# A long convolution with gated projections on one core: a hand-written order replaced by a list scheduler, with the head's products taken from PSUM, six first-stage groups set aside and late gating of four chunks

## The chip, the core and the metric

The kernel runs on one core of a Trainium2 chip. TensorE (PE) multiplies, with its weight loads shown as a row of their own (PEld); VectorE (DVE), ScalarE (ACT) and GpSimd (POOL) work on elements; SyncE (SP) issues the transfers, which 16 DMA engines carry out. Matmul results land in PSUM, eight banks of 128 x 512 numbers; everything else lies in SBUF. Each engine takes its own instructions in program order. The metric is device time in microseconds (us) of one execution. All data is 32-bit float.

## The reference

For 8 batches of 6400 steps and 128 channels: a causal convolution of each channel with a filter as long as the sequence (by FFT in the reference), a five-tap causal convolution of the result whose sigmoid is a gate, a projection, the gating, and a second projection.

```python
L = 2 * S
Xf = np.fft.rfft(x, n=L, axis=1)
Hf = np.fft.rfft(h, n=L, axis=0)
y = np.fft.irfft(Xf * Hf[None, :, :], n=L, axis=1)[:, :S, :]
...
for k in range(K):
    gate_pre += conv_w[k][None, None, :] * xp[:, k:k + S, :]
gate = 1.0 / (1.0 + np.exp(-gate_pre))
val = x @ w_val
return (gate * val @ w_out).astype(np.float32)
```

In the last lines `x` is the convolution's `y`, and `xp` is it with four zero steps in front. The transfer of a batch in and out is 3.3 MB each way.

## The kernel before

The 6400 steps are laid out as 100 x 64, and the Fourier transform is done as four stages of matmuls.

- **First stage** (`Forward.group`, 16 groups of 8 channels a batch): four matmuls of 128x200 against `r1_sb`, from an input tile `x`. Four copies of 64x400 bring the result from PSUM to `gy` (for the filter `h` to `gh`, which lies in `dt`).
- **Second stage** (`s2_mm`, 13 blocks `kb` of 8 frequencies, the last of 4): a matmul of 128x128 per frequency against the loaded `m2`. `Product` multiplies by the filter's spectrum: `swap` brings the swapped parts to `w` (two ACT instructions, one with the sign), `mul_u` and `mul_t` (DVE) multiply by the two spectrum tiles `h`, and `add` sums into `gy` (POOL; the last block on DVE).
- **Third stage** (`s3_quad`, 32 quads of 4 channels): four matmuls of 128 columns from `gy` against `r3_sb`, and one copy of 100x512 to `dt`, on ACT and DVE in turn.
- **Fourth stage** (`Chunk`, 13 chunks: the head chunk of 4 columns, and 12 of 5): two matmuls of 100 columns per column from `dt` against `m4_sb`, into one bank. From that bank `copies` (ACT) takes the result `y`, the first tap into the gate's cells (in `dt` or `gl`) and a scaled copy `p`; `taps` adds three taps on DVE and one on POOL. Then `project` (one matmul of up to 500 columns from `y`), `sigm` (ACT), `gate` (DVE), `output` (a second matmul, from the gated cells) and `store`: a copy to `y` and a transfer out.

The **head** of the program does the first stage for `h` and for batch 0, and then their second stages in turn. There `Spectrum` copies each block of the filter's spectrum twice (ACT the real part, DVE the imaginary part) to tiles of 128 partitions, which the product uses and which are stored to HBM (`hd`); for blocks from `LATER` = 7 on only half is stored, and `h_double` copies it to the other half later.

Then each batch `b` runs its third stage, with the first stage of batch `b + 1` beside it (two quads, then a group), and its fourth stage, with the second stage of batch `b + 1` beside it: in step `s` of the loop at L551 chunk `s` and block `s + 1`. A chunk is projected two steps after it is made; what is left of a batch at the end (`trail`, L583) is done in the first rounds of the next third stage. The order on each engine is the order of the calls, which `_InOrder` keeps. PSUM is two pairs of banks and four single banks (before the first batch: four pairs). All transfers are issued by SP, in the order of the calls.

Of the kernel before, what the change touches and what calls it, by code (L numbers as in the profile page):

```python
# [15 lines left out]
C = 128  # L16
# [17 lines left out]
LATER = 7  # L34
# [3 lines left out]
XB = 4  # L38

# [60 lines left out]

@with_exitstack
def longconv_moe(ctx: ExitStack, tc: tile.TileContext, x, h, r1, m2, r3, m4, w64, out):
# [6 lines left out]
    ps2 = ctx.enter_context(tc.tile_pool(name="ps2", bufs=2, space=bass.MemoryType.PSUM))  # L109
    psp = tc.tile_pool(name="psp", bufs=2, space=bass.MemoryType.PSUM)  # L110
    pairs = [ps2, psp.__enter__()]
# [5 lines left out]
    m4_sb = cp.tile([PX, N2 + 1, N1], F32, name="m4_sb")  # L117
# [5 lines left out]
    yl = {a: cp.tile([128, n, N1], F32, name=f"yl_{a}") for a, n in CHUNKS if a >= LATE}  # L123
# [4 lines left out]
    p_t = [cp.tile([128, CH, N1], F32, name=f"p_{i}") for i in range(2)]  # L128
    hd = dp.tile([NKB, 2, 2 * N2, KB * C], F32, name="hd")

    def weights():
        ti = gl.rearrange("p n t -> p (n t)")[:, : 3 * NW].bitcast(I32)
        tf = gl.rearrange("p n t -> p (n t)")[:, 3 * NW : 6 * NW]
        nc.sync.dma_start(ti[:, : 2 * NW], w64.bitcast(I32))
        w = ti[:, : 2 * NW].rearrange("p (n two) -> p two n", two=2)
        lo, hi = w[:, 0], w[:, 1]
        a = ti[:, 2 * NW :]
        f, g = tf[:, :NW], tf[:, NW : 2 * NW]
        b = tf[:, 2 * NW :].bitcast(I32)
        v = nc.vector  # L140

        def bits(o, i, s, p):
            v.tensor_scalar(out=o, in0=i, scalar1=s, scalar2=None, op0=p)

        yield
        bits(a, lo, 28, ALU.logical_shift_right)
        yield
        bits(a, a, 15, ALU.bitwise_and)
        yield
        bits(b, hi, (1 << 20) - 1, ALU.bitwise_and)  # L150
        yield
        v.tensor_copy(g, b)
        yield
        bits(b, a, 1, ALU.logical_shift_right)
        yield
        bits(a, a, 1, ALU.bitwise_and)
        yield
        v.tensor_copy(f, a)
        yield
        v.scalar_tensor_tensor(out=g, in0=g, scalar=8.0, in1=f, op0=MUL, op1=ALU.add)  # L160
        yield
        v.tensor_copy(f, b)
        yield
        v.tensor_tensor(out=g, in0=g, in1=f, op=ALU.add)
        yield
        v.tensor_scalar(out=g, in0=g, scalar1=2.0**-23, scalar2=1.0, op0=MUL, op1=ALU.add)
        yield
        bits(a, hi, 20, ALU.logical_shift_right)
        yield
        bits(a, a, 2047, ALU.bitwise_and)  # L170
        yield
        v.tensor_copy(f, a)
        yield
        v.tensor_scalar(out=f, in0=f, scalar1=-896.0, scalar2=0.0, op0=ALU.add, op1=ALU.max)
        yield
        v.tensor_scalar(out=f, in0=f, scalar1=255.0, scalar2=None, op0=ALU.min)
        yield
        v.tensor_copy(a, f)
        yield
        bits(a, a, 23, ALU.logical_shift_left)  # L180
        yield
        bits(b, hi, 31, ALU.logical_shift_right)
        yield
        bits(b, b, 31, ALU.logical_shift_left)
        yield
        v.tensor_tensor(out=a, in0=a, in1=b, op=ALU.bitwise_or)
        yield
        v.tensor_tensor(out=w_sb, in0=g, in1=a.bitcast(F32), op=MUL)
        yield

    act = nc.scalar.copy
    dve = nc.vector.tensor_copy

    def pair():
        pairs.append(pairs.pop(0))
        return pairs[-1].tile([128, 2, 512], F32, name="pt2", tag="pt2")

    def single():
        return ps1.tile([128, 512], F32, name="pt1", tag="pt1")

    class Forward:


        def __init__(self, src, dst):
            self.src, self.dst, self.n, self.i = src, dst, 0, 0

        def load(self, n=1):
            for _ in range(n):
                if self.n < NG:
                    nc.sync.dma_start(x_sb[self.n % XB], self.src[self.n])  # L210
                    self.n += 1

        def group(self):
            g = self.i
            self.i += 1
            t = x_sb[g % XB]
            pt = pair()
            for m in range(4):
                nc.tensor.matmul(
                    pt[:, m // 2, (m % 2) * SW : (m % 2) * SW + 2 * N1],  # L220
                    lhsT=t[:N1, 2 * m : 2 * m + 2, :].rearrange("p j n -> p (j n)"),
                    rhs=r1_sb,
                    start=True,
                    stop=True,
                )
            self.load()
            v = pt.rearrange("p b (m x) -> p b x m", x=SW)
            return [
                lambda e, j=j, c=c: e(
                    self.dst[c * N2 : (c + 1) * N2, 4 * g + 2 * j : 4 * g + 2 * j + 2],  # L230
                    v[j * N2 : (j + 1) * N2, :, c * N1 : (c + 1) * N1],
                )
                for j in range(2)
                for c in range(2)
            ]

    def count(kb):
        return min(KB, N1 - kb * KB)

    def m2_load(kb):  # L240
        if kb < NKB:
            n = count(kb)
            nc.sync.dma_start(m2_sb[kb % M2B][:, :n], m2[:, kb * KB : kb * KB + n])

    def h_load(kb):
        if kb < NKB:
            n = count(kb) * C
            for r in range(2):
                nc.sync.dma_start(h_sb[(2 * kb + r) % HB][:, :n], hd[kb, r, :, :n])

    def h_double(kb):
        n = count(kb) * C
        for r in range(2):
            nc.sync.dma_start(hd[kb, r, N2:, :n], hd[kb, r, :N2, :n])

    def kdt(t, kb):
        n = count(kb)
        return t[:, : n * C].rearrange("p (d k t) -> p d k t", k=n, t=2)

    def s2_mm(src, kb):  # L260
        pt = pair()
        n = count(kb)
        for k in range(n):
            nc.tensor.matmul(
                pt[:, k // 4, (k % 4) * C : (k % 4 + 1) * C],
                lhsT=m2_sb[kb % M2B][:, k, :],
                rhs=src[:, :, kb * KB + k],
                start=True,
                stop=True,
            )  # L270
        if n <= 4:
            return pt[:, 0, : n * C].rearrange("p (k d t) -> p d k t", t=2, d=C // 2)
        return pt.rearrange("p b (k d t) -> p d (b k) t", t=2, d=C // 2)

    hx = h_sb + [dt[:, N1 * C + i * KB * C : N1 * C + (i + 1) * KB * C] for i in range(2)]

    class Spectrum:
        def __init__(self, kb):
            self.kb, self.v = kb, s2_mm(gh, kb)
            self.h = [hx[(2 * kb + r) % len(hx)] for r in range(2)]  # L280

        def real(self):
            t = kdt(self.h[0], self.kb)
# [346 lines left out]
```

## Time and profile before

| | us |
|---|---|
| median of three runs (1117.69 to 1118.20) | 1117.95 |
| span of the profiled execution | 1115.5 |
| busy: PE, DVE, ACT, POOL | 1053.5, 831.8, 729.7, 410.7 |

The profiled execution's own time is its span and 2.4 us around it, if it ran at the median. The profile gives idle time of an engine with the instruction that released it ("releaser"), groups of instructions by operation and tile (buffer numbers left out, so `pt` is any PSUM tile and `h` any of the spectrum tiles; `m2_sb`, `m4_sb` and `r3_sb` are shown as `m`, `m_sb` and `r_sb`), a timeline in which equal instructions that follow each other are merged ("x16"), and windows: stretches of the span with the busy time of each engine. A matmul of 32-bit floats shows as two records, so that 8 matmuls are x16. All matmul instructions have one line, that of the wrapper at L89, and are told apart by their tiles.

### The profile page before, as it was taken

To read this page: it belongs to the slowest core of one execution; us is meant where nothing else is said; L and a number is where in the kernel's file an instruction comes from. 1 tells how busy PE (TensorE), PEld (TensorE's weight loads), DVE (VectorE), ACT (ScalarE), POOL (GpSimd) and SP (SyncE) were. 2 spreads that over 40 slices of the span, in tenths; PEclk is the share of its full clock that TensorE was granted. 3 is DMA by queue.
4 is the path that set the end of the run, shared out by engine and by line. 5 is a ranking of instruction groups with operands and counts; after the bars stand their busy time and mean duration, and the time that the engine had idled before them with its cause. 6 is when DMAs were issued, how large, how long until landed. Compare 5 with 4: busy or idle time off the path is not lost.

```text
span 1115.5 us, 19581 instructions
## 1 busy us (share of the span) xinstructions
PE 1053.5 (94%) x7480; PEld 942.9 (85%) x7480; DVE 831.8 (75%) x1176; ACT 729.7 (65%) x1188; POOL 410.7 (37%) x220
## 2 busy tenths in 40 slices
PE   8987799989999899999999899998999899998997
PEld 8986799769998699878998699886998689986975
DVE  6799677985599665995579855996569956797375
ACT  5798257864498446974588555984568744885365
POOL 0044104850078301870048500882028700584022
PEclk9999799999999999999999999999999999999999
DMA  5696956965199733976279651997249661892012
GB/s 151 210 329 189 328 169 228 305 191 202 34 325 283 250 93 119 335 218 237 59 240 314 210 170 49 335 277 243 82 148 333 193 236 50 283 300 76 18 33 86
DMA packets 109259, 221.15 MB, mean 198 GB/s; under 512 B 45290, under 2 KB 53454, under 8 KB 109006
## 3 DMA queue, kind: packets, MB, share of 16 engines
q1 hardware_dynamic: 109166, 219.89, 61.4%
q8 instruction: 60, 0.98, 0.4%
q14 instruction: 33, 0.27, 0.1%
HBM read 183.42 MB, written 39.32 MB: 200 GB/s over the span
## 4 chain that ended last, share of the span: by engine, by line
PE 82%; ACT 9%; DVE 5%; issue 2%; DMA 1%; POOL 0%; POOLq 0%; ACTq 0%; SPq 0%; DVEq 0%
PE pt L89 82%; ACT yl L89 2%; ACT w L89 2%; ACT dt L89 2%; DVE w L89 1%; ACT p L89 1%; DVE gy L89 1%; ACT gl L89 1%; ACT gy L89 1%; DVE h L89 1%; DVE dt L89 1%; DVE gl L89 0%; DMA x<-xl 0%; DMA x<-hl 0%; POOL dt L89 0%
## 5 line engine op out<-in xcount | busy, mean ns | idle before, releaser
L89 POOL TENSOR_TENSOR gy<-gy,w 128x1024 f32<-128x1024 f32 x96 | 227.9, 2374 | 147.6 <-DVE w L89 145.1
L89 PEld LDWEIGHTS pt<-m_sb,dt 100*128 100x128 f32 x2048 | 243.3, 192 | 43.0 <-issue 32.7
L89 ACT COPY dt<-pt 100x512 f32<-100x512 f32 (+3 forms) x280 | 163.1, 583 | 164.4 <-PE pt L89 163.1
L89 PEld LDWEIGHTS pt<-r_sb,gy 128*100 128x100 f32 x2048 | 240.0, 172 | 30.3 <-issue 20.0
L89 PE MATMUL pt<-r_sb,gy 128*100 128x128 f32 x2048 | 247.7, 274 | 15.2 <-DVE gy L89 8.9
L89 PE MATMUL pt<-m_sb,dt 100*128 100x100 f32 x2048 | 243.7, 274 | 3.5 <-DVE dt L89 2.6
L89 PE MATMUL pt<-r_sb,x 100*128 100x200 f32 x1152 | 216.7, 336 | 4.9 <-DMA x<-hl 4.3
L89 PEld LDWEIGHTS pt<-gy,m 128*128 128x128 f32 x1600 | 194.5, 188 | 23.5 <-issue 9.9
L89 DVE COPY dt<-pt 100x512 f32<-100x512 f32 (+2 forms) x168 | 116.7, 695 | 124.4 <-PE pt L89 121.9
L89 PE MATMUL pt<-gy,m 128*128 128x128 f32 x1600 | 201.7, 279 | 2.1 <-DVE dt L89 1.6
L89 PEld LDWEIGHTS pt<-r_sb,x 100*128 100x128 f32 x1152 | 193.5, 192 | 5.1 <-issue 4.3
L89 ACT COPY gy<-pt 64x400 f32<-64x400 f32 x256 | 124.4, 486 | 101.0 <-PE pt L89 98.7
L89 DVE COPY gy<-pt 64x400 f32<-64x400 f32 x256 | 146.5, 572 | 44.5 <-PE pt L89 41.9
L89 POOL MEMSET dt<- 128x4 f32 x8 | 0.8, 104 | 422.9 <-PE pt L89 422.9
L89 DVE TENSOR_TENSOR gy<-pt,h 128x1024 f32<-128x1024 f32 (+1 forms) x100 | 117.5, 1175 | 45.1 <-ACT w L89 44.1
L89 DVE SCALAR_TENSOR_TENSOR dt<-pt,w_sb,dt 128x500 f32<-128x500 f32 (+7 forms) x216 | 132.6, 630 | 11.4 <-POOL dt L89 5.3
L89 ACT ACTIVATE w<-pt 64x1024 f32<-64x1024 f32 (+1 forms) x104 | 102.7, 988 | 41.6 <-PE pt L89 40.4
L89 DVE SCALAR_TENSOR_TENSOR gl<-pt,w_sb,gl 128x500 f32<-128x500 f32 (+2 forms) x168 | 108.8, 651 | 22.1 <-issue 9.9
L89 DVE TENSOR_TENSOR w<-w,h 128x1024 f32<-128x1024 f32 (+1 forms) x100 | 122.4, 1224 | 0.0
L89 POOL TENSOR_TENSOR dt<-dt,p 128x500 f32<-128x500 f32 (+1 forms) x64 | 101.4, 1585 | 52.5 <-DVE dt L89 40.5
L89 PE MATMUL pt<-dt,w_sb 128*128 128x500 f32 (+2 forms) x240 | 115.3, 571 | 1.2 <-ACT dt L89 1.2
L89 POOL TENSOR_TENSOR gl<-gl,p 128x500 f32<-128x500 f32 (+1 forms) x48 | 83.2, 1734 | 74.7 <-DVE gl L89 73.7
(31 smaller groups left out, 715.9 us busy)
## 6 DMA issues: line engine op xcount, KB each, us to landing
h<-hd SPq DMA_DIRECT2D x168, 512.0 KB, 6.3
m<-m SPq DMA_DIRECT2D x96, 512.0 KB, 6.0
x<-xl SPq DMA_DIRECT2D x128, 224.0 KB, 2.8
out<-dt SPq DMA_DIRECT2D x56, 250.0 KB, 5.9
out<-yl SPq DMA_DIRECT2D x40, 250.0 KB, 3.1
hd<-h SPq DMA_DIRECT2D x10, 512.0 KB, 5.0
x<-hl SPq DMA_DIRECT2D x16, 224.0 KB, 2.6
h<-hd SPq DMA_DIRECT2D x14, 256.0 KB, 4.7
```

The lines of the kernel that those rows point to most:

```text
L89: return self._tc.keep_in_program_order(call(*args, **kwargs))
```

## The change

The calls no longer issue instructions. Each step is an `_Op` with a cost per engine that may do it, its predecessors and its PSUM bank; `_Plan.order` goes through time with these costs, gives each free engine the ready operation that is due first, and gives out the eight banks; then the operations are issued in the order in which they began. `due` follows from a base that the code sets for each step and from what comes before. Where two engines may do a step (copies of the first and third stage, output copies), the scheduler picks.

```python
HEAD_END = 101000
PERIOD = 126600
THIRD = 57000
...
LAGS = 8200
...
def fits(o, e):
    if o.port and e in ("vector", "gpsimd") and port > now:
        return False
    if any(max(free[x], now) + c[1] < now + o.cost[e][1] for x, c in o.cost.items() if x != e):
        return False
    b = o.bank
    if b is None:
        return True
    if o.new:
        return all(x.spot is not None for x in b.before) and self.room(b, halves, now) is not None
    return not any(x != e and s & o.side and t > now for x, s, t in b.seen)
```

`port` marks DVE operations with both inputs in SBUF and POOL's additions; the scheduler never starts one of them on one of the two engines while one runs on the other.

**The head.** ACT makes the two real copies and one imaginary copy with the sign turned, POOL makes the other imaginary half from it, and the products read PSUM, without `swap`:

```diff
-            act(t[:N2], self.v[:N2])
-            act(t[N2:], self.v[:N2])
-            dve(t[:N2], self.v[N2:])
-            dve(t[N2:], self.v[N2:])
+        r0 = add(lambda e: nc.scalar.copy(t[0][:N2], v()[:N2]), cost, [p, *old[0]], bank=bank)
+        r1_ = add(lambda e: nc.scalar.copy(t[0][N2:], v()[:N2]), cost, [p, *old[0]], bank=bank)
+        i0 = add(lambda e: nc.scalar.activation(t[1][:N2], v()[N2:], AF.Copy, scale=-1.0), cost, [p, *old[1]], bank=bank)
+            lambda e: nc.gpsimd.tensor_scalar(out=hs[1][N2:, :n], in0=hs[1][:N2, :n], scalar1=-1.0, scalar2=None, op0=MUL),
...
+            nc.vector.tensor_tensor(out=t[:N2], in0=v()[N2:], in1=hi[:N2], op=MUL)
+            nc.vector.tensor_tensor(out=t[N2:], in0=v()[:N2], in1=hi[N2:], op=MUL)
```

Five blocks (`WHOLE`, seven before) are stored whole, the others by half and doubled later. The first 32 input loads have twelve buffers instead of four, eight of them in the space of `m4_sb`.

**Six groups aside.** Groups 0 to 5 of batch 1's first stage (`STASH`) are computed in the head into the space of `m4_sb`; under the third stage of batch 0, POOL copies each (128x800) to `gy` when the quads that read its place are done, and `m4` is loaded after that.

**Late gating and the y ring.** Of chunks 9 to 12 (`LAGGED`) only the copy `y` is taken from PSUM; the first tap, the scaled copy and the taps read `y`. Their base, and that of the gates, lies beside the next third stage. `y` lies in a ring of six tiles (and one for the head chunk); in the last batch seven tiles of `w` and `h` join it.

```diff
+            lag = i >= LAGGED
+            if lag and nxt:
+                plan.base = fourth + PERIOD - THIRD - 15000 + LAGS * (i - LAGGED)
+                v = to if lag else pv()
...
-                    self.more(j, o, self.p[:, i : i + o.shape[1]])
+                        nc.vector.scalar_tensor_tensor(out=o, in0=v(), scalar=wc(j), in1=o, op0=MUL, op1=ADD)
```

How the instructions stand now, at three places. In these rows a trailing "x4" is a count of matmuls, `pt_...` and `ps_...` are PSUM tiles, `m_0` to `m_3` the tiles of `m2`, and x_85 to x_90 input tiles. PE at the end of the head, before: the last blocks of the filter (`dt`) and batch 0 (`gy`), then the third stage (`r_sb,gy`).

```order
L89 MATMUL pt_724<-dt,m_3_82 128x128 x8
L89 MATMUL pt_744<-gy,m_2_81 128x128 x8
L89 MATMUL pt_753<-dt,m_0_79 128x128 x4
L89 MATMUL pt_769<-gy,m_3_82 128x128 x8
L89 MATMUL pt_789<-gy,m_0_79 128x128 x4
L89 MATMUL pt_818<-r_sb,gy 100x128 x4
L89 MATMUL pt_823<-r_sb,gy 100x128 x4
L89 MATMUL pt_828<-r_sb,x_87 128x200 x4
```

And now:

```order
L101 MATMUL ps_94<-dt,m_3_80 128x128 x8
L101 MATMUL ps_95<-gy,m_3_80 128x128 x8
L101 MATMUL ps_97<-dt,m_0_77 128x128 x4
L101 MATMUL ps_94<-gy,m_0_77 128x128 x4
L101 MATMUL ps_96<-r_sb,x_87 128x200 x4
L101 MATMUL ps_97<-r_sb,x_88 128x200 x4
L101 MATMUL ps_96<-r_sb,x_85 128x200 x4
L101 MATMUL ps_95<-r_sb,x_86 128x200 x4
L101 MATMUL ps_94<-r_sb,gy 100x128 x60
L101 MATMUL ps_95<-r_sb,x_87 128x200 x4
```

Four groups of batch 1 (`r_sb,x`) stand between the last block and the third stage; two more stand between earlier blocks, and fifteen quads follow each other before the next group.

DVE in the rounds of the head, before: two copies of the imaginary part, then the products of a block, with `w` made by ACT.

```order
L89 COPY h_86<-pt_515 64x1024 x2
L89 TENSOR_TENSOR gy<-pt_535,h_83 128x64x16
L89 TENSOR_TENSOR w_91<-w_91,h_84 128x1024
L89 COPY dt<-pt_545 64x1024 x2
L89 TENSOR_TENSOR gy<-pt_565,h_85 128x64x16
L89 TENSOR_TENSOR w_92<-w_92,h_86 128x1024
```

And now:

```order
L101 TENSOR_TENSOR gy<-ps_97,h_81 128x64x16
L101 TENSOR_TENSOR w_89<-ps_97,h_82 64x1024 x2
L101 TENSOR_TENSOR gy<-ps_94,h_83 128x64x16
L101 TENSOR_TENSOR w_90<-ps_94,h_84 64x1024 x2
L101 TENSOR_TENSOR gy<-ps_96,dt 128x64x16
L101 TENSOR_TENSOR w_91<-ps_96,dt 64x1024 x2
```

Three products from PSUM are left for a block (the second row counts two of 64 partitions); the copies are gone.

PE at the seam from the fourth stage of one batch to the third stage of the next, before: the last two chunks (`m_sb,dt`) with projections from `yl`, `gl` and `dt`.

```order
L89 MATMUL pt_1716<-yl_76,w_sb 128x500
L89 MATMUL pt_1718<-m_sb,dt 128x100 x10
L89 MATMUL pt_1729<-gl,w_sb 128x500
L89 MATMUL pt_1745<-yl_77,w_sb 128x500
L89 MATMUL pt_1747<-gl,w_sb 128x500
L89 MATMUL pt_1766<-r_sb,gy 100x128 x4
L89 MATMUL pt_1771<-r_sb,gy 100x128 x4
L89 MATMUL pt_1776<-r_sb,x_87 128x200 x4
L89 MATMUL pt_1788<-yl_78,w_sb 128x500
L89 MATMUL pt_1790<-gl,w_sb 128x500
L89 MATMUL pt_1796<-r_sb,gy 100x128 x4
```

And now (the same place after batch 1):

```order
L101 MATMUL ps_95<-m_sb,dt 128x100 x10
L101 MATMUL ps_95<-y_70,w_sb 128x500
L101 MATMUL ps_96<-m_sb,dt 128x100 x10
L101 MATMUL ps_96<-dt,w_sb 128x500
L101 MATMUL ps_94<-y_71,w_sb 128x500
L101 MATMUL ps_94<-r_sb,gy 100x128 x4
L101 MATMUL ps_94<-gl,w_sb 128x500
L101 MATMUL ps_94<-r_sb,gy 100x128 x8
L101 MATMUL ps_95<-r_sb,x_85 128x200 x4
L101 MATMUL ps_94<-y_72,w_sb 128x500
```

The last two chunks now stand with one projection of an earlier chunk (`y_70`, `y_71`) and one second projection, and the projections of chunks 9 to 12 (from `y_72` on) come after the third stage's start, between its quads and groups.

More of the change, by code (lines that the diff above doesn't have):

```diff
@@ L33 @@
 LATE = 35
-LATER = 7
+LAGGED = 9
+WHOLE = 5
+STASH = 6
 M2B = 4
@@ L98, in __init__, with ap @@
         self.gpsimd, self.sync = (_InOrder(tc, e) for e in (nc.gpsimd, nc.sync))
+class _Bank:
+    def __init__(self, n):
+        self.n, self.place = n, None
+    def ap(self):
+        return self.place
+class _Op:
+    def __init__(self, run, cost, after, bank=None, new=False, side=3, port=False):
+        self.run, self.cost, self.bank, self.new, self.side, self.port = run, cost, bank, new, side, port
+        self.after = [a for a in after if a is not None]
+        self.rank = self.at = self.done = self.engine = None
@@ L159, in weights @@
[L159 to L173, printed above, removed]
@@ L187, in weights @@
[L187 to L218, printed above, removed]
+            return lambda e: v.tensor_scalar(out=o, in0=i, scalar1=s, scalar2=None, op0=p)
@@ L219, in group, with m2_load, second, mm @@
+    m2_in, m2_user = [], []
+    def m2_load(kb):
+        n, k = len(m2_in), count(kb)
+        after = m2_user[n - M2B] if n >= M2B else []
+        m2_in.append(dma(m2_sb[n % M2B][:, :k], m2[:, kb * KB : kb * KB + k], 64 * k, after, 6000))
+        m2_user.append([])
+        return n
+    def second(src, kb, slot, after, bank):
+        def mm(e):
+            for k in range(count(kb)):
                 nc.tensor.matmul(
-                    pt[:, m // 2, (m % 2) * SW : (m % 2) * SW + 2 * N1],
@@ L225, in group @@
                 )
[L226 to L243, printed above, removed]
@@ new lines, in longconv_moe @@
+    for kb in range(NKB):
+        plan.where = f'head {kb}'
+        plan.base = 46300 + 3680 * kb
+        m2_load(kb)
+        p, hs, re, im, st = spectrum(kb)
+        bank = _Bank(2)
+        plan.base += 2760
+        q = second(gy, kb, kb, xs1, bank)
+        a, b, c = direct(kb, q, bank, hs, re, im)
+        hx_user += [[a, st[0]], [b, st[1]]]
+        head_done += [p, a, b, *st]
+        adds.append(c)
+    stashed = first_stage(x[1], stash_at, lambda g: [*firsts[: 2 * NG]], HEAD_END - 1000, 1350, range(STASH)) if B > 1 else []
@@ L251, in h_double @@
[L251 to L273, printed above, removed]
@@ new lines, in longconv_moe @@
+        adds = []
+        if nxt:
+            for kb in range(NKB):
+                plan.where = f's2 b{b+1} {kb}'
+                plan.base = fourth + SECOND * kb
+                slot = m2_load(kb)
+                h_load(kb)
+                bank = _Bank(2)
+                p = second(gy, kb, slot, ys1, bank)
+                hs = [h_sb[(len(h_in) - 2 + r) % HB] for r in range(2)]
+                a, m, c = product(kb, p, bank, hs, h_in[-2:])
+                h_user += [a, m]
+                adds.append(c)
@@ L588, in _lay_x @@
+        gated(len(CHUNKS) - 1)
+        gated(0)
+        dt_old = [*s4_new, *dt_new]
+    plan_ops = plan.order(places)
+    for op in plan_ops:
+        op.run(op.engine)
 def _lay_x(v):
```

854 lines of the change are left out of this document (560 added, 294 removed).

## The prediction

> **What bounds the kernel now.** First the span and the busy shares, then the chain that ended last.
>
> ```profile
> span 1115.5 us, 19581 instructions
> PE 1053.5 (94%) x7480; PEld 942.9 (85%) x7480; DVE 831.8 (75%) x1176; ACT 729.7 (65%) x1188; POOL 410.7 (37%) x220
> ```
>
> ```profile
> PE 82%; ACT 9%; DVE 5%; issue 2%; DMA 1%; POOL 0%; POOLq 0%; ACTq 0%; SPq 0%; DVEq 0%
> ```
>
> TensorE is busy for 94% of the span and carries 82% of the chain. So time is to be had only where PE waits or runs slowly, and I cut the span at the first third-stage product of each batch. A row of the windows gives a stretch, its length, the busy time of PE, weight load, DVE, ACT and POOL, the granted clock, and the DMA share and GB/s.
>
> ```profile
> 4.35:50.30 45.95, 45.43 (x256) 45.14 (x257) 35.47 (x62) 29.17 (x60) 0.00 (x0) 1.00 0.61 179
> 50.30:118.67 68.37, 49.19 (x401) 47.02 (x401) 64.06 (x55) 52.68 (x56) 28.47 (x12) 0.94 0.78 253
> 118.67:246.53 127.86, 123.53 (x884) 112.34 (x885) 101.16 (x156) 84.29 (x136) 51.12 (x26) 0.98 0.74 243
> 246.53:375.70 129.17, 125.05 (x895) 111.55 (x894) 96.63 (x138) 85.78 (x141) 52.37 (x27) 1.00 0.65 207
> 1021.59:1115.50 93.91, 85.03 (x577) 69.02 (x575) 50.79 (x82) 47.65 (x89) 16.61 (x16) 0.97 0.15 46
> ```
>
> The first row is the first stage of `h` and batch 0, the second their second stages with the products (the head), the third batch 0, the fourth one of six equal batches (129.17), the last is batch 7. PE is 72% busy in the head, 97% in a batch. What PE would need without a wait is read from starts that follow each other in its timeline.
>
> ```profile
> 124.47 1.91 PE L89 MATMUL pt<-r_sb,gy 128*100 128x128 f32 x16
> 126.22 1.52 PE L89 MATMUL pt<-r_sb,x 100*128 100x200 f32 x8
> 127.58 1.91 PE L89 MATMUL pt<-r_sb,gy 128*100 128x128 f32 x16
> ```
>
> ```profile
> 177.07 2.37 PE L89 MATMUL pt<-m_sb,dt 100*128 100x100 f32 x20
> 179.28 3.90 PE L89 MATMUL pt<-gy,m 128*128 128x128 f32 x32
> 183.01 2.37 PE L89 MATMUL pt<-m_sb,dt 100*128 100x100 f32 x20
> ```
>
> ```profile
> 239.49 1.10 PE L89 MATMUL pt<-yl,w_sb 128*128 128x500 f32 x2 [1.41 <-ACT yl L89]
> 244.75 1.10 PE L89 MATMUL pt<-yl,w_sb 128*128 128x500 f32 x2 [1.08 <-ACT yl L89]
> 245.69 1.00 PE L89 MATMUL pt<-gl,w_sb 128*128 128x500 f32 x2
> 246.53 1.04 PE L89 MATMUL pt<-r_sb,gy 128*100 128x128 f32 x8
> ```
>
> Two quads of the third stage (8 products) take 126.22 - 124.47 = 1.75, a first-stage group 1.36, so 16 rounds take 49.8. Five columns of the fourth stage take 179.28 - 177.07 = 2.21, two second-stage blocks 3.73 (1.865 each), a projection 0.84 (0.67 for 400 columns). A batch has 64 columns (28.3), 12.5 blocks (23.3) and 24 + 2 projections (21.5). Together 122.9: **each batch loses 6.3**. Who makes PE wait is summed over the span:
>
> ```profile
> PE pt L89 <- ACT yl L89: 19.1, 20, 1.4
> PE pt L89 <- ACT dt L89: 9.4, 15, 1.2
> ```
>
> 28.5 us, four per seam, sit where the last chunks' copies on ACT come late; 1.41 and 1.08 of them are in the rows above.
>
> **The change, part by part.**
>
> *Head rounds.* One round, on all engines:
>
> ```profile
> 84.00 1.23 DVE L89 TENSOR_TENSOR gy<-pt,dt 128x1024 f32<-128x1024 f32 x1
> 85.14 1.22 DVE L89 TENSOR_TENSOR w<-w,dt 128x1024 f32<-128x1024 f32 x1
> 86.34 2.03 ACT L89 COPY dt<-pt 64x1024 f32<-64x1024 f32 x2 [0.77 <-PE pt L89]
> 86.39 2.49 DVE L89 COPY h<-pt 64x1024 f32<-64x1024 f32 x2
> 88.90 1.23 DVE L89 TENSOR_TENSOR gy<-pt,h 128x1024 f32<-128x1024 f32 x1
> 89.13 2.09 PE L89 MATMUL pt<-dt,m 128*128 128x128 f32 x16 [0.97 <-DVE h L89]
> ```
>
> DVE starts its product at 84.00 and again at 88.90: 4.9 a round, made of 2.49 of copies, 1.23 and 1.22, without a gap, and PE waits 0.97 for it. The change takes the two copies and the product of the swapped part away from DVE and the swap from ACT; DVE gets three products from PSUM (by 1.22, 3.65 a round), ACT three half copies (half of 2.03 each, 3.0), POOL a negation beside its add. PE needs 2 x 1.865 = 3.73 and becomes the bound, if nothing else does. From 50.30 to the end of the last block (108.63 + 1.16 = 109.79) is 59.5; 25 blocks at 1.865 are 46.6. Gain 12.9.
>
> The negation (64x1024, one input) is in no row. Bounds: nothing, or as much as the two-input add of 2.37, which would make POOL's round 4.75. The Trainium skill, GPSIMD Engine Reference, section 4.1 (Engine selection), calls one-input work on GpSimd roughly line-rate against about half speed for two inputs; by it, as an estimate, the negation costs some 1.2 and POOL's round is 3.6, and the sum below would stand. DMA is the other unknown:
>
> ```profile
> 80.00:90.00 10.00, 8.09 (x68) 7.74 (x67) 9.83 (x9) 8.31 (x9) 4.75 (x2) 1.00 0.95 322
> ```
>
> It is 95% busy at 4.9 a round. Five blocks instead of seven are now stored whole, and the doubling of the other eight is partly queued inside the head.
>
> *Six groups aside.* After the last block PE waits 8.88 for the products' end and restarts slowly:
>
> ```profile
> 108.63 1.16 PE L89 MATMUL pt<-gy,m 128*128 128x128 f32 x8 [1.62 <-DVE dt L89]
> 118.67 3.71 PE L89 MATMUL pt<-r_sb,gy 128*100 128x128 f32 x16 [8.88 <-DVE gy L89]
> 122.17 2.47 PE L89 MATMUL pt<-r_sb,x 100*128 100x200 f32 x8
> ```
>
> 16 records take 3.50 to the next start instead of 1.75, and the first group 2.30 instead of 1.36: 2.7 lost. Now six groups of batch 1 (6 x 1.36 = 8.1) stand there. So the third stage of batch 0 begins at 50.3 + 46.6 + 8.1 = 105.0 plus a rest for the end of the chain and for the unknowns. The rest lies between 0 and 13 (13 rounds of 4.75 instead of 3.73). I take 4, near POOL's add of 2.37 (the row further down) plus a last short DVE add: **109.0 instead of 118.67**. The six copies back run on POOL under the third stage; m4's loads wait for them, with over 20 us before the fourth stage reads m4.
>
> *Batch 0.* 127.86 - 2.7 (slow start) - 8.1 (groups done) - 5.0: the projections that stand behind the next third stage's start go from three of 500 and two of 400 columns (3.9) to nine and two (8.9). That is 112.1; less the 2.4 below, **109.7**.
>
> *The seam, six batches.* Chunks 9 to 12 now give their bank back after one copy (ACT), and their taps read the copy in SBUF under the next third stage:
>
> ```profile
> 375.70:430.97 55.27, 54.19 (x395) 51.47 (x394) 31.79 (x52) 25.83 (x51) 1.24 (x1) 1.00 0.43 144
> 430.97:504.89 73.92, 70.87 (x500) 60.10 (x501) 64.93 (x86) 59.94 (x91) 51.12 (x26) 1.00 0.80 254
> ```
>
> There, DVE is busy 31.8 of 55.3 and ACT 25.8; in the fourth stage 64.9 and 59.9 of 73.9. Three taps and a gate move for each of four chunks (12 x 0.74 + 4 x 0.67 = 11.6 on DVE, some 8 on ACT). ACT also takes nearly all copies of the third stage, 15 more a batch:
>
> ```profile
> L89 ACT COPY dt<-pt 100x512 f32<-100x512 f32 x128 | 74.9, 585 | 149.5 <-PE pt L89 148.6
> ```
>
> 15 x 0.585 = 8.8, and DVE loses as many. ACT then works about 43 of 58 there (49.8 + 8.9 of PE work), DVE about 33: hidden. Without that cover ACT's 8.8 would go onto PE. The seam's two long waits (1.41 + 1.08) should go; the smaller ones and the changes between stages stay. Bounds: nothing gained, or all 6.3. I take 2.4, the two waits: **126.8 x 6 = 760.8**. Below nothing is the slow rival.
>
> A weighing against the change: the moved taps have both inputs in SBUF.
>
> ```profile
> 114.88 2.37 POOL L89 TENSOR_TENSOR gy<-gy,w 128x1024 f32<-128x1024 f32 x1 [1.47 <-DVE w L89]
> 115.23 2.57 DVE L89 TENSOR_TENSOR w<-w,h 128x512 f32<-128x512 f32 x1
> ```
>
> ```profile
> L89 POOL TENSOR_TENSOR gl<-gl,p x48: 818/1808/2098, 219.1 to 1107.4; 128x500 f32<-128x500 f32 x40, 128x300 f32<-128x300 f32 x8
> ```
>
> The DVE product of half width began at 115.23, ended at 117.80, and needs 0.69 alone: it stood until POOL's add ended at 117.25. POOL's adds of 300 to 500 columns reach from 0.82 to 2.10. So the two shut each other out. Twelve taps a batch may each meet a POOL operation; if each lost half of 2.37 on average, DVE would get 14 us more in the third stage, 47 of 58, still covered. The Trainium skill, SBUF — State Buffer, section Who interferes with whom, says so: a DVE instruction with two SBUF inputs and a GpSimd instruction that reads SBUF block each other wholly, for the instruction's length. The rows agree (2.57 against 0.69). By that rule a tap can lose a whole operation, 28 us instead of 14, and DVE (61 of 58) would run out of cover: a way into the second rival.
>
> *Last batch.* 93.91 + 5.0 of projections moved in. Its waits:
>
> ```profile
> 1055.37 6.47 PE L89 MATMUL pt<-m_sb,dt 100*128 100x100 f32 x56 [0.88 <-DVE dt L89]
> 1067.51 2.67 PE L89 MATMUL pt<-m_sb,dt 100*128 100x100 f32 x20 [1.73 <-DVE dt L89]
> ```
>
> 0.88 + 1.73 = 2.6 may go, since its chunks get seven more buffers; the closing chain of taps, gate, projection and store stays. **96.3**.
>
> *Other edits.* The y ring of six replaces in-place cells and own tiles: copies of the same size, and a store must land before its buffer's next use six chunks later, over 25 us. PSUM as eight banks given out by the scheduler adds no instruction. The order of SP changes most: stores, h and m2 loads are queued in planned order, each waiting in turn.
>
> Sum: 109.0 + 109.7 + 760.8 + 96.3 = 1075.8, against the span 1115.5. The runs' median, 1117.95, lies 2.4 above it: **1078**.
>
> **The rivals.**
>
> *Head bound by POOL or DMA.* Rounds of 4.75: 9 more than my rest, **1087**. For it: DMA at 95%. Against: stores fall by two blocks' halves and three h buffer pairs give slack.
>
> *Only the head gains.* A list fixed from rounded durations shifts waits instead of removing them, or the lock eats the cover; batches stay at 129.2: 7 x 2.4 = 17 more, **1095**. For it: PE is already 97% busy in a batch.
>
> *Better than thought.* Half of the remaining 3.9 goes too, about 124.1 a batch: 7 x 2.7 = 19 less, **1059**. For it: DVE and ACT have over 20% free in every stage by the windows.
>
> *Slower: a store in front of a load.* SP takes its queue in order, and output stores now stand between the h loads of the fourth stage.
>
> ```profile
> h<-hd SPq DMA_DIRECT2D x168, 512.0 KB, 6.3
> ```
>
> An h pair is read by two products (1.23 + 1.22) and reloaded in 6.3: 8.8 in all, so two pairs serve a block every 4.4, against 65 us of PE work for 13 blocks, 5.0 each. A store that waits d for its chunk holds up each load behind it: (8.8 + d)/2 passes 5.0 at d = 1.2, and from d = 2.1 a batch grows by 6.0 (13 x 0.46), which over seven batches eats the whole gain. At d = 2.5 it is 13 x 0.65 = 8.5 a batch, 59 in all: **1137**. Against it: before, the stores stood in the same queue, and PE's waits name no h load.
>
> **How the numbers follow.** Forecast 1078 with 0.50, head only 0.17, better 0.12, head bound 0.10, slower 0.08, and 0.03 that gains and new waits cancel. The measurement tells apart some 0.2% (2 us), which is my bound for no change. Faster: 0.50 + 0.17 + 0.12 + 0.10 = 0.89; the same 0.03; slower 0.08. The range takes in 1059 and 1095 and the forecast's neighbours, a rest of 0 to 13 in the head and 0 to 6.3 a batch short of their far ends: 1058 to 1102. Left out are the slow rival, the 0.03 and some 0.07 at both ends.
>
> **What would show it.** Head: second-stage blocks of `dt` should follow each other in about 3.7 instead of 4.9, and the first third-stage product start at 105 to 113, its 16 records taking about 1.9, without a slow start; POOL's negations in the lines near 1.2. Batch: start to start 124 to 128, with PE's waits for ACT at the seam under 15 us in the sum of waits (28.5 now), none for h loads. ACT should be busy for some 45 us more than now (118 copies by 0.585, less about 24 swaps by 1.0), DVE some 80 less (118 by 0.69 and the head's copies, less 24 cross products). The prediction is wrong if PE waits for stores or loads on SP, if the lock makes DVE the last releaser in the third stage, or if the batches stay at 129.

## The result and the profile after

The changed kernel takes **1382.01 us** (median of four runs, 1374.47 to 1393.47), the kernel before 1118.05 beside it: 1.2372 times as long, with a 95% interval of 1.2309 to 1.2435. The forecast was 1078, and the range ended at 1102. From the page of the profiled run:

```profile
span 1372.7 us, 19881 instructions
PE 1154.0 (84%) x7480; PEld 979.3 (71%) x7480; DVE 757.2 (55%) x1069; ACT 774.8 (56%) x1269; POOL 419.0 (31%) x239
```

PE is busy for 1154.0 of 1372.7, so it waits for 218.7, against 62.0 before. That is 157 of the 257 us between the two spans; in the other 100 PE's own records, as many as before (7480), last longer. A quad on its own shows 1.12 in the lines below, against 0.87 from start to start before, and the granted clock was 0.951 over the run, against 0.992; how the 100 divide between the two isn't shown. DVE (757.2) and ACT (774.8) did what was forecast, -75 and +45, and no engine has become the bound: beside PE each has less than 60%. So work that was meant to lie side by side stands in a row. The windows show where: the head, batch 0's third and fourth stage, and the same two of batch 1 (columns as in the prediction).

```profile
50.97:123.80 72.83, 59.71 (x449) 57.67 (x449) 53.05 (x54) 48.65 (x61) 63.11 (x25) 0.95 0.77 245
123.80:184.02 60.22, 46.78 (x337) 42.54 (x337) 10.24 (x18) 26.82 (x51) 5.13 (x6) 1.00 0.53 173
184.02:268.14 84.12, 71.05 (x492) 60.82 (x492) 59.84 (x77) 56.49 (x81) 42.18 (x23) 0.96 0.74 248
268.14:341.57 73.43, 62.09 (x405) 53.65 (x404) 29.14 (x48) 39.00 (x76) 4.97 (x4) 1.00 0.26 81
341.57:422.94 81.37, 71.02 (x488) 59.73 (x489) 60.81 (x79) 53.94 (x78) 43.07 (x23) 0.96 0.78 259
```

Batch 0 starts at 123.80 instead of the forecast 109.0. Its third stage takes 60.2 and batch 1's 73.4 (52.6 and 55.3 before), their fourth stages 84.1 and 81.4 (75.2 and 73.9 before). By the starts of the batches the 257 us of the two spans come from the head (+5), batch 0 (+16), the six equal batches (154.6 to 160.7 each instead of 129.2, together +169) and the last batch (160.5 instead of 93.9, +67).

Two patterns make up the third stage. The first is how batch 0's begins, in the timeline (rows of PE and ACT):

```profile
123.80 1.97 PE L101 MATMUL ps<-r_sb,gy 128*100 128x128 f32 x16 [2.71 <-DVE gy L101]
125.85 0.59 ACT L101 COPY dt<-ps 100x512 f32<-100x512 f32 x1 [1.84 <-issue]
126.49 1.12 PE L101 MATMUL ps<-r_sb,gy 128*100 128x128 f32 x8 [0.72 <-ACT dt L101]
127.65 0.59 ACT L101 COPY dt<-ps 100x512 f32<-100x512 f32 x1 [1.21 <-PE ps L101]
128.29 1.12 PE L101 MATMUL ps<-r_sb,gy 128*100 128x128 f32 x8 [0.68 <-ACT dt L101]
129.45 0.59 ACT L101 COPY dt<-ps 100x512 f32<-100x512 f32 x1 [1.21 <-PE ps L101]
130.09 1.12 PE L101 MATMUL ps<-r_sb,gy 128*100 128x128 f32 x8 [0.68 <-ACT dt L101]
131.25 0.59 ACT L101 COPY dt<-ps 100x512 f32<-100x512 f32 x1 [1.21 <-PE ps L101]
131.89 1.12 PE L101 MATMUL ps<-r_sb,gy 128*100 128x128 f32 x8 [0.68 <-ACT dt L101]
```

From the third on every quad takes 1.80, where the prediction had read 0.87 between starts. Within the 1.80 a quad's products (1.12, then 0.04) and one copy on ACT (0.59, then 0.05) follow each other strictly, though the quads have two banks to alternate between. The last batch's third stage, quads and projections without groups, goes at the same pace: 65.8 instead of 33.8. The waits in the program say why. PE counts its matmuls on one semaphore, and the scheduler gave the two halves of the place `ps_94` to quads in turn:

```
ACT copies half 0 of ps_94: waits for PE 360, the last product into half 1
ACT copies half 1 of ps_94: waits for PE 364, the last product into half 0, of the next quad
ACT copies half 0 of ps_94: waits for PE 368, the last product into half 1, of the next quad
```

The halves are different banks but one tile, and the waits are set for the tile as a whole: a reader of one half waits for every product that was issued ahead of it into the other half too, and the next products wait for that reader. The trace agrees: the first two quads end at 125.77, and the copy of the first one begins only then, at 125.85, after ACT has stood idle for 1.84. Call this **the tie**.

The second pattern is the steady round of two quads and one group, here in batch 1 (rows of PE, ACT and DVE):

```profile
309.69 1.07 ACT L101 COPY dt<-ps 100x512 f32<-100x512 f32 x2 [0.77 <-PE ps L101]
310.23 1.59 PE L101 MATMUL ps<-r_sb,x 100*128 100x200 f32 x8 [0.57 <-issue]
311.65 1.91 PE L101 MATMUL ps<-r_sb,gy 128*100 128x128 f32 x16
311.85 0.98 ACT L101 COPY gy<-ps 64x400 f32<-64x400 f32 x2 [1.09 <-PE ps L101]
312.87 1.17 DVE L101 COPY gy<-ps 64x400 f32<-64x400 f32 x2 [2.75 <-ACT gy L101]
313.60 1.07 ACT L101 COPY dt<-ps 100x512 f32<-100x512 f32 x2 [0.77 <-PE ps L101]
314.14 1.59 PE L101 MATMUL ps<-r_sb,x 100*128 100x200 f32 x8 [0.57 <-issue]
```

A round takes 313.60 - 309.69 = 3.91 instead of 3.11. All groups have one place, and all that this place goes through stands in a row: 1.6 of products, 0.98 of ACT's copies of one half of the partitions, 0.04, 1.17 of DVE's copies of the other half, 0.1, the next group. The scheduler had counted the two copies side by side, since they read different partitions of the banks. In the trace DVE's start only when ACT's end, and the sum of waits has that as a row of its own:

```profile
DVE gy L101 <- ACT gy L101: 284.2, 100, 28.0
```

A place that is handed out again in the moment in which the scheduler believes it free has no slack for this. Its rule was the first free place, and for a single bank first of all the half beside one in use; so one place was used in every round, while others stood empty.

The head has another cause. POOL alone there:

```profile
56.33 2.77 POOL L101 TENSOR_SCALAR h<-h 64x1024 f32<-64x1024 f32 x1 [55.89 <-ACT h L101]
59.43 2.77 POOL L101 TENSOR_SCALAR h<-h 64x1024 f32<-64x1024 f32 x1 [0.33 <-ACT h L101]
62.28 2.38 POOL L101 TENSOR_TENSOR gy<-gy,w 128x1024 f32<-128x1024 f32 x1
64.75 2.77 POOL L101 TENSOR_SCALAR dt<-dt 64x1024 f32<-64x1024 f32 x1
67.59 2.37 POOL L101 TENSOR_TENSOR gy<-gy,w 128x1024 f32<-128x1024 f32 x1
...
118.94 1.49 POOL L101 TENSOR_SCALAR h<-h 64x512 f32<-64x512 f32 x1
120.51 2.37 POOL L101 TENSOR_TENSOR gy<-gy,w 128x1024 f32<-128x1024 f32 x1
```

Negation and add alternate: 2.77 + 2.37 with two short gaps are 5.3 a round. POOL is busy for 63.1 of the 66.6 from 56.33 to 122.88, and batch 0 starts 0.9 behind the end of its last add.

### The profile page after: what moved, and what is told of

The parts are those of the page before. It is cut to its first block, busy times and chain, and to the rows that moved or that the text cites. A ratio compares the mean times of both kernels' runs of the same rounds, so it can differ in the third digit from the quotient of the medians.

```text
span 1372.7 us, 19881 instructions
## 1 busy us (share of the span) xinstructions
PE 1154.0 (84%) x7480; PEld 979.3 (71%) x7480; DVE 757.2 (55%) x1069; ACT 774.8 (56%) x1269; POOL 419.0 (31%) x239
## 5 line engine op out<-in xcount | busy, mean ns | idle before, releaser
L101 PEld LDWEIGHTS ps<-r_sb,gy 128*100 128x100 f32 x2048 | 244.8, 173 | 100.9 <-ACT dt L101 37.9
L101 PEld LDWEIGHTS ps<-m_sb,dt 100*128 100x128 f32 x2048 | 258.7, 205 | 78.3 <-ACT w L101 16.8
L101 PE MATMUL ps<-r_sb,gy 128*100 128x128 f32 x2048 | 263.0, 278 | 51.4 <-ACT dt L101 22.5
L101 PE MATMUL ps<-m_sb,dt 100*128 100x100 f32 x2048 | 266.2, 290 | 42.1 <-ACT w L101 14.2
L101 DVE COPY gy<-ps 64x400 f32<-64x400 f32 x242 | 139.4, 576 | 287.9 <-ACT gy L101 284.2
L101 ACT COPY dt<-ps 100x512 f32<-100x512 f32 (+2 forms) x286 | 160.7, 588 | 185.6 <-PE ps L101 164.0
L101 PE MATMUL ps<-r_sb,x 100*128 100x200 f32 x992 | 196.4, 344 | 46.6 <-issue 35.5
L101 PEld LDWEIGHTS ps<-gy,m 128*128 128x128 f32 x1600 | 195.2, 190 | 33.3 <-issue 16.0
L101 PEld LDWEIGHTS ps<-r_sb,x 100*128 100x128 f32 x992 | 169.7, 194 | 66.3 <-issue 55.9
L101 PE MATMUL ps<-gy,m 128*128 128x128 f32 x1600 | 204.1, 281 | 12.8 <-DVE gy L101 5.6
L101 ACT ACTIVATE w<-ps 64x1024 f32<-64x1024 f32 (+1 forms) x91 | 90.0, 989 | 84.1 <-DVE gy L101 47.8
L101 POOL TENSOR_TENSOR gl<-gl,q 128x500 f32<-128x500 f32 (+1 forms) x48 | 56.7, 1181 | 242.7 <-DVE gl L101 242.7
```

Of the source, the lines that this page charges most:

```text
L101: return self._tc.keep_in_program_order(call(*args, **kwargs))
```

## The experiments

**Theory A**: the loss in the batches comes from the tie, and from places handed out first-free, without slack. **B**: the engines themselves fall behind (the negation, the lock between DVE and POOL, ACT with all third-stage copies, the moved taps). **C**: DVE's half of a group behind ACT's half is all of it. **D**, for the head: POOL's negation bounds it; its rival **E** is the DMA share, or the chain behind the last block. A time without an interval is that of a single run; the four runs of the changed kernel lie within 1.4% of each other, the eight of e1_untied within 0.6%.

**Untied, longest free** (e1_untied). From the third stage on, two places stay for two-bank users; the other four banks become four tiles. So users of one bank and of two no longer share places, which was also so in the kernel before.

```diff
+        if b.n == 2:
+            free = [(max(p), i, 0) for i, p in enumerate(halves[:2] if b.late else halves) if all(t is not None and t <= now for t in p)]
+        else:
+            free = [(p[h], i, h) for i, p in enumerate(halves) for h in (0, 1) if i > 1 and p[h] is not None and p[h] <= now]
+        return min(free)[1:] if free else None
...
+            one.extend(pr.tile([128, 512], F32, name=f"pt_{k}") for k in range(4))
```

> Change: from the third stage on, the two-bank users get two places of their own, and the one-bank users four tiles of one bank each, at the addresses of the other two places; of the free ones the one free longest is given out. Everything else is as in the changed kernel. Theory A (the two halves of one place are ordered as one tile, so that a quad's copy waits for the next quad's products in the other half, and a place that comes free is given out at once): the 15 quads at the start of batch 0's third stage fall from 1.80 us each to 0.9 to 1.0, the rounds of two quads and a group from 3.91 to 3.1 to 3.3, a batch from 154.8 to 126 to 132, the whole to 1095 to 1135 us. The head stays (first third-stage product near 123). Rival B (the engines themselves fall behind: POOL's negation of 2.77, DVE's product from SBUF of 1.42 instead of 1.25, ACT with all third-stage copies, taps of the last four chunks under the next third stage): none of these is touched, the rounds stay at 3.9 and the whole above 1300.

Measured: 1113.85 us (ratio to before 0.996, 0.9945 to 0.9976), 268 less than the changed kernel, with the instructions of DVE, ACT and POOL the same to within three. PE with the 15 quads of batch 0 (120 records), and then PE, ACT and DVE in a round of a later batch:

```profile
125.41 13.27 PE L101 MATMUL pt<-r_sb,gy 128*100 128x128 f32 x120
```

```profile
672.95 1.91 PE L101 MATMUL pt<-r_sb,gy 128*100 128x128 f32 x16
673.15 0.98 ACT L101 COPY gy<-ps 64x400 f32<-64x400 f32 x2 [0.77 <-PE ps L101]
674.16 1.17 DVE L101 COPY gy<-ps 64x400 f32<-64x400 f32 x2 [1.94 <-ACT gy L101]
674.70 1.52 PE L101 MATMUL ps<-r_sb,x 100*128 100x200 f32 x8
676.05 0.71 PE L101 MATMUL pt<-r_sb,gy 128*100 128x128 f32 x5
```

15 quads take 13.27: 0.88 each. A round takes 676.05 - 672.95 = 3.10. DVE's copies still start behind ACT's, but nobody waits for that place now. So B falls for the batches.

**One engine for each group** (e2_one_engine).

```diff
-            for j in range(2):
+            for _ in range(1):
...
-                    for c in range(2):
+                    for j, c in ((0, 0), (0, 1), (1, 0), (1, 1)):
```

> Change: the four copies of a first-stage group are one step on one engine (ACT or DVE), instead of two copies on each. Theory C (the loss comes from DVE's half of a group waiting for ACT's half, 284 us of waits in 100 places): those waits vanish and so does most of the loss: under 1200 us. Theory A (halves tied, a place given out again at once): a group's place is then held for 1.5 of products + 0.1 + 2.0 to 2.3 of copies + 0.1 = 3.7 to 4.0, as long as the 0.98 + 0.04 + 1.17 in a row take now, so a round with that place alone stays near 3.9 and the first 15 quads at 1.80; the waits of DVE for ACT vanish, and the whole falls little, to 1300 to 1370 us. Rival B (slow engines): unchanged, 1372.

1323.63 us, 58 less. DVE's waits for ACT are gone, and batch 0's quads still take 1.80 each. The time is inside A's range, and C, which needed less than 1200, falls as the whole cause. But A's round near 3.9 did not come: in batch 2 rounds take 3.1 to 3.4 (groups at 455.13, 458.50 and 461.88). The list now counts a group's four copies one behind the other, as they run, and its order has the groups in two places in turn (`ps_95` and `ps_96`). So the second pattern came from a place given out too early by the list's count.

**Longest free, still tied** (e3_rotate).

```diff
-        one = [(i, p.index(True)) for i, p in enumerate(ok) if any(p)]
-        return min(one, key=lambda x: (all(ok[x[0]]), x[0]), default=None)
+        one = [(p[h], i, h) for i, p in enumerate(halves) for h in (0, 1) if ok[i][h]]
+        return min(one)[1:] if one else None
```

> Change: of the free places, or halves, the one that came free longest ago is given out, instead of the first. The halves stay halves of one tile. Theory A says that giving a place out at once and the tie between halves both cost: the 15 quads no longer share one place, so they fall to 0.9 to 1.2 each; rounds near 3.1 to 3.5; what the tie costs in the fourth stage, where chunks and projections sit beside each other, stays. 1170 to 1280 us. If only the choice of the place matters: as e1_untied, below 1135. If only the tie matters: above 1330. Rival B: 1372.

1206.87 us, as A expected. The 15 quads take 0.89 each. In batches 1 to 6 third stages fall to 59.4 to 61.3, close to the 59.2 to 60.5 of e1_untied, but fourth stages stay at 78 to 83, where those of e1_untied take 68 to 70: what is left of the tie's price lies there, where chunks and projections still share tiles.

**The scheduler knows of the tie** (e4_tie_known).

```diff
-                            for k in (0, 1) if b.n == 2 else (h,):
+                            for k in (0, 1):
```

> Change: the scheduler gives a one-bank user a whole place (its other half stays empty until it is done) and takes the place free longest; so nothing in its list is tied that it does not know of, but it has four places instead of up to eight halves. Theory A: near e1_untied, 1110 to 1150 us, with 15 quads at 0.9 to 1.0 each. If the tie did not matter, fewer places could only cost: as e3_rotate or slower. Rival B: 1372 or more.

1123.9 us, with only four places, and the 15 quads at 0.99 each. So what matters is less the number of tiles than that the list and the waits agree on what is free.

**Untied, first free** (e7_untied_first).

```diff
-        return min(free)[1:] if free else None
+        return min(f[1:] for f in free) if free else None
```

> Change: e1_untied, but of the free places the first is given out, as in the changed kernel, instead of the one free longest. It completes a square: halves tied or not, first or longest free (1382 for tied and first, 1207 for tied and longest, 1114 for untied and longest). Theory A (both cost): 1130 to 1200 us, rounds of 3.1 to 3.5. If the tie alone were the cause, 1114; if the first-free choice alone kept the rounds at 3.9, above 1300.

1171.2 us. The round with one place for all groups is back, without the tie:

```profile
702.48 1.59 PE L101 MATMUL ps<-r_sb,x 100*128 100x200 f32 x8 [0.57 <-issue]
703.91 1.91 PE L101 MATMUL pt<-r_sb,gy 128*100 128x128 f32 x16
704.11 0.98 ACT L101 COPY gy<-ps 64x400 f32<-64x400 f32 x2 [1.58 <-PE ps L101]
705.12 1.17 DVE L101 COPY gy<-ps 64x400 f32<-64x400 f32 x2 [2.74 <-ACT gy L101]
706.39 1.59 PE L101 MATMUL ps<-r_sb,x 100*128 100x200 f32 x8 [0.57 <-issue]
```

706.39 - 702.48 = 3.91, so this pattern belongs to the choice of the place. The time is inside A's range, but its rounds of 3.1 to 3.5 did not come, and rounds of 3.91 do not make more than 1300 either. The square:

| us | first free | longest free |
|---|---|---|
| tied | 1382 | 1207 |
| untied | 1171 | 1114 |

The tie costs 211 or 93, the first-free choice 175 or 57; each is worse with the other. The untied runs also keep users of one bank and of two apart, so the two rows differ by that as well; e4_tie_known, where all share the four places, speaks for the tie.

**The copy of the other sign on ACT**, in the untied kernel (e5_untied_act) and alone in the changed one (e6_act_alone):

```diff
-            lambda e: nc.gpsimd.tensor_scalar(out=hs[1][N2:, :n], in0=hs[1][:N2, :n], scalar1=-1.0, scalar2=None, op0=MUL),
-            {"gpsimd": (1250, 1250)}, [i0, *old[1]],
+            lambda e: nc.scalar.copy(t[1][N2:], v()[N2:]),
+            cost, [p, *old[1]], bank=bank,
```

> Change: e1_untied, and in the head the copy of the swapped part with the other sign is made by ACT from PSUM (a half copy of 1.0) instead of by POOL's negation from SBUF (2.77). Theory D (POOL bounds the head: 2.77 + 2.37 and two short gaps = 5.3 a round against PE's 3.73): ACT then has four half copies, 4.05 a round, POOL 2.4; the first third-stage product starts at 125.4 - 13 x (5.3 - 4.1) = 110, between 104 and 114, and the whole falls from 1113.9 to 1094 to 1102 us; batches stay at 127.4. Rival E (the head is bound by the DMA share of 0.75 to 0.95, or by the chain product, add, first third-stage product): start stays at 120 or later, whole within 4 us of 1113.9.

> Change: the changed kernel with only the negation moved to ACT as in e5_untied_act; places and halves as in the changed kernel. Theory D: the first third-stage product starts 11 to 18 us earlier, at 106 to 113; theory A: the batches stay at 144 to 156 each, so the whole stays above 1345 us. If POOL's negation had caused the slow batches too, it would fall below 1250.

1104.32 us (0.9875, 0.9854 to 0.9896) and 1350.9 us. The first third-stage product starts at 110.82 and 112.80 (125.41 and 123.80 without), and alone it leaves the batches slow (142 to 159 each). The head's window in e1_untied and in e5_untied_act:

```profile
50.97:125.41 74.44, 61.67 (x455) 59.64 (x454) 53.10 (x55) 47.41 (x59) 63.05 (x25) 0.91 0.75 241
```

```profile
50.97:110.82 59.85, 54.90 (x433) 52.13 (x432) 51.70 (x52) 56.69 (x64) 28.53 (x12) 1.00 0.88 298
```

POOL falls from 63.1 to 28.5, the head by 14.6, at a DMA share that rises from 0.75 to 0.88: D, not E. ACT is now busy for 56.7 of 59.9 and probably the next bound, which no run tests. The whole fell by 9.5 and not by the 12 or more expected, since batch 0 then took 117.4 instead of 115.2, and the six batches behind it 3.3 more together, one of them 132.7.

**No chunk gated late** (e8_no_lag), on e5_untied_act:

```diff
-LAGGED = 9
+LAGGED = 13
```

> Change: e5_untied_act with all twelve chunks gated in the fourth stage (no chunk's taps and gate moved under the next third stage). The prediction gave this part 2.4 us a batch (17 us over seven seams): 1112 to 1118 us by that. If it is worth the whole of what a batch of before lost (6.3): up to 1142. If the moved taps' lock with POOL ate it: no slower than e5_untied_act.

1180.96 us: 77 more, beyond every size that was named. Batches 1 to 6 take 136.7 to 140.4, where the order made by hand, in which only the last projections are late, takes 129.2. So the late gates are worth some 11 a batch to this list, but nearly all of it makes good what the list itself loses: without them its third stages take 58 to 59 instead of 55.3, and its fourth stages 78 to 82 instead of 73.9.

**No groups aside** (e11_no_stash2), on e5_untied_act.

```diff
-STASH = 6
+STASH = 0
...
-                m4_load(ys1, begin + 14000)
+                m4_load(firsts[: 2 * NG], begin + 14000)
```

In a first version without the second edit (e10_no_stash, 1141.47 us) m4's loads came ahead of first-stage loads into the same buffer, so it computes something else and its time isn't used. Mended:

> Change: e5_untied_act with no first-stage group of batch 1 kept aside, the loads of m4 held back until the first stages are done. By the prediction's terms: PE waits about 8.9 behind the last block and restarts slowly (2.7), while six groups of 8.1 go back into batch 0's third stage: 11.6 more than e5_untied_act, 1114 to 1118 us. If the waits among the four groups that stand there now (1.26, 0.81, 0.39, 0.68 in e5_untied_act) and the copies back eat half of it: 1107 to 1112. If the groups set aside are worth nothing: within 3 us of 1104.

1105.58 us (0.9891, 0.9856 to 0.9926), against 1104.32: no difference to be measured. PE's timeline behind the last block:

```profile
100.96 1.19 PE L101 MATMUL ps<-gy,m 128*128 128x128 f32 x8 [0.49 <-DVE w L101]
108.25 5.31 PE L101 MATMUL pt<-r_sb,gy 128*100 128x128 f32 x24 [6.10 <-DVE gy L101]
113.39 1.52 PE L101 MATMUL ps<-r_sb,x 100*128 100x200 f32 x8
```

The wait (6.10) and the slow restart are there (24 records in 5.1 instead of 2.6), but the third stage begins at 108.25, 2.6 earlier than with the groups in front of it. Batch 1 starts at 231.47 instead of 228.19, so 3.3 of the 11.6 are left there, and later differences between batches hide them.

**Columns earlier** (e9_chunks_earlier), on e5_untied_act.

```diff
-EARLY = -1800
+EARLY = 2500
...
-                done.append(add(ev, cost, [p, *before(g)], bank=bank, side=1 << j))
+                done.append(add(ev, cost, [p, *before(g)], bank=bank))
```

> Change: e5_untied_act; the scheduler is also told that two engines' reads of one bank take turns whatever their partitions, and a chunk's columns are due 2.5 us before their share of the fourth stage begins instead of 1.8 us behind it. Theory F (in a batch of e5_untied_act, 128.7 long with 124.6 of PE work, the 4.1 of waits come from DVE and POOL finishing a chunk's taps and a block's products late; columns that stand earlier leave them more time): batches 125 to 127.5, whole 1080 to 1097 us, below every version so far. Rival G (these waits only move, as the seam's did: 4.1 a batch before and 4.1 after): batches 128 to 130, whole 1100 to 1110.

1096.26 us (0.9804, 0.9788 to 0.9821): the fastest of all, 2% below the kernel before. Its batches 1 to 6, 127.2 to 128.6, lie between F's and G's: the waits became a little shorter (3.7 in the batch from 482.77, 128.00 long) and did not go. Which of the two edits did this isn't shown.

**The tie in an order made by hand.** The ring of the kernel before, made of halves (e12_before_tied) and of four tiles in the same fixed turn (e13_before_ring).

```diff
+    ring = [t[:, h] for t in [ps1.tile([128, 2, 512], F32, name=f"pt1_{i}") for i in range(2)] for h in range(2)]
...
+        ring.append(ring.pop(0))
+        return ring[-1]
```

> Change: the kernel before, order and all else as it was, but its ring of four one-bank tiles is made of the halves of two tiles of two banks, in turn. Theory A (the halves of one tile are ordered as one tile): where the products of a quad are issued ahead of the copy of the quad in the other half, that copy waits for them; quads fall to 1.80 each, a round of two quads and a group to 3.9 to 5.0 instead of 3.1, and chunks and projections in the fourth stage wait for each other's readers too: 1250 us or more. If the tie is harmless and only the list scheduler's order is at fault: 1118.

> Change: e12_before_tied with four tiles of one bank each in the same fixed turn, so that only the tie is gone. As there, a chunk's bank is given out again before its taps have read it, so the outputs differ from the reference's. If the tie made the time of e12_before_tied (1659): below 1350 us, with a fourth stage under 100 instead of 137 us. If the fixed turn made it: 1550 or more. The third stage took 58 there against 55 before, so it should stay within 5 us of 55 either way.

1659.17 and 1350.19 us. Both leave out a wait of the kernel before, since a chunk's bank is given out again before its taps have read it; so they compute something else, and their prices hold for this fixed turn alone. Of the 541 above the kernel before, 309 go with the tie and 232 with the fixed turn; 1350.19 lies at the very edge of what was expected for the tie. In batches 1 to 6 the third stage takes 58 to 63 with the tie and 58 to 59 without it, so the expected quads of 1.80 were wrong for this order. The fourth stage takes 133 to 138 with the tie and 97 to 101 without it. The granted clock fell as well, to 0.837 over the run with the tie and 0.909 without it, and is part of these prices.

## Why the prediction was wrong

**The step that failed** stands among the other edits: "PSUM as eight banks given out by the scheduler adds no instruction". PE's records are as many as before, and so it was costed at nothing. The way in which the banks were given out, the tie and the first-free choice together, cost 268 us (1382.01 to 1113.85). Instructions were counted, but not the waits that follow from the tile in which an operand lies and from how soon its bank is handed on. No rival and none of the signs named this; the slow rival looked to SP, and in the sum of waits no row of PE names an `h` load. The order of PE's rows in the section on the change had the sign: groups in `ps_95` and quad after quad in `ps_94`, where before each had a tile of its own (`pt_818`, `pt_823`, `pt_828`).

**The negation**, "Bounds: nothing, or as much as the two-input add of 2.37". The upper end was too low, 2.77, and with it the rival "Head bound by POOL or DMA" came true, on POOL, and by more than its 9: 123.80 instead of 109.0. With ACT in POOL's place it is 110.82, so the other terms of that start (25 blocks, six groups, a rest of 4) were 1.8 short together. The Trainium skill, GPSIMD Engine Reference, section 4.1 (Engine selection), calls one-input work on GpSimd roughly line-rate; the estimate from it was 1.2, and the trace disagrees for this operation, at 2.77.

**Six groups aside.** The wait and the slow restart are there without them (6.10 + 2.5 in e11_no_stash2, for 8.88 + 2.7 before), and batch 0 does restart at full pace (16 records in 1.97 at 123.80). But what was booked as gain is not measurable in the whole, 1104.32 against 1105.58.

**Batch 0, "109.7".** 115.2 in e1_untied: 5.5 short, with places untied. PE is busy for 109.1 of it and waits for 6.1; 2.7 of that is one wait for a load of `m2`, which no term of the forecast has, and 3.2 are waits for DVE.

**The seam, "I take 2.4, the two waits".** A steady batch of e1_untied, its third stage and then the whole of it, and PE's waits in it, with its waits for ACT in the same stretch of the kernel before (634 to 763) ahead of them:

```profile
627.12:687.60 60.48, 59.28 (x407) 53.79 (x406) 29.92 (x49) 40.05 (x75) 4.97 (x4) 1.00 0.34 107
627.12:755.79 128.67, 124.54 (x896) 111.55 (x895) 90.37 (x125) 93.95 (x154) 47.26 (x27) 1.00 0.62 208
```

```profile
PE pt L89 <- ACT yl L89: 2.8, 3, 1.4
PE pt L89 <- ACT dt L89: 1.2, 2, 0.7
```

```profile
PE ps L101 <- DVE gy L101: 1.4, 2, 0.8
PE pt L101 <- POOL gy L101: 1.2, 1, 1.2
PE pt L101 <- ACT dt L101: 0.7, 1, 0.7
```

The batch is 128.67 long with 124.54 of PE work; before it was 129.18 with 125.06 (634.06 to 763.24). PE waits for 4.1 in both. The waits for ACT fell from 4.0 to 0.7, and others, for DVE and POOL above all, took their place. So the six batches are the rival "Only the head gains" even untied: 0.5 a batch, not 2.4. The cover which that step counted on was there: in the third stage ACT works 40.05 of 60.48 and DVE 29.92, against 43 and 33 of 58 forecast.

**The lock** cost nothing that shows in the third stage: in e1_untied POOL works only 4.97 of the 60.48, and the moved taps take 0.73 to 0.76. In the fourth stage of the changed kernel the product `w<-w,h` takes 1418 ns on average (1250 before) and POOL's adds `gl<-gl,q` of 500 columns 1252 (1744 before), as if DVE now stood more often and POOL less; no run tests this.

**Last batch, "96.3".** 98.5 in e1_untied, from 1013.23 to 1111.7.

Together, for e1_untied: 125.4 + 115.2 + 772.6 + 98.5 = 1111.7, against 109.0 + 109.7 + 760.8 + 96.3. The four terms were 16.4, 5.5, 11.8 and 2.2 too low, 36 in all; the other 261 of the changed kernel's span are the places. So without the failed step the time would have been 1114: still above the range. With the negation on ACT as well it is 1104.32, 2 above the range's end.

Of the signs that the prediction named, these came: no slow start, no wait for `h` loads, ACT +45, DVE -75. These did not: blocks of `dt` 3.7 apart (4.6, from 50.97 to 108.11 in 12.5 rounds), the start between 105 and 113, negations near 1.2, batches of 124 to 128, and PE's waits for ACT under 15 (27.1 for `dt` and 13.2 for `y` in the changed kernel's sum of waits).

## What to carry to other kernels

Before a planned order is trusted, set what it counts as side by side against the waits that the program really has, buffer by buffer: two halves of one tile may be one thing to the waits, and a plan that doesn't know it is late everywhere at once. Give out the buffer that has been free longest; first-free leaves no slack for any error in the plan. An edit that adds no instruction may add a wait to many of them.

## What the runs showed of the hardware

- One-input work on POOL has no single price: in the changed kernel the negation of 64x1024 takes 2766 ns, more than the two-input add of 128x1024 in the kernel before (2374), but the copy of 128x800 takes 856.
- ACT's and DVE's copies from different partitions of the same banks never ran at once in the rounds shown; DVE's start 0.03 or 0.04 behind ACT's end. The Trainium skill, PSUM — Partial Sum Buffer, section PSUM bank collisions raise a hardware error, says that two engines on different quadrants of one bank run clean, and calls ordering by bank the simple version. Here the program's waits order them, so no run shows whether the chip would do both at once.
- The granted clock did not follow PE's busy share alone. In the changed kernel it stayed at 1.00 in third stages in which PE was busy for 46.78 of 60.22 and 62.09 of 73.43, and was 0.96 in fourth stages with 71.05 of 84.12 and 71.02 of 81.37. It was 0.78 in this fourth stage of e12_before_tied, in which PE was busy for 97.95 of 134.54:

```profile
367.79:502.33 134.54, 97.95 (x500) 77.32 (x501) 66.36 (x87) 60.37 (x91) 51.03 (x26) 0.78 0.47 147
```
